# Identity products and split stores in the opening, attention-times-v in runs of two head pairs, and the first w3 columns converted during the attention

## The chip, the cores and the metric

The kernel runs on 1 core of a Trainium2 chip. The time is the device time of one execution in microseconds; the kernel before took 1345.91 us as the median of three runs.

## The reference

Inputs: q, k, v of 4 batches x 12 heads x 448 positions x 64, two 12 x 12 matrices that mix heads, and the weights of two layers.

```python
scores = scale * (q @ k.T)                      # per batch and head
scores = einsum('bhij,hg->bgij', scores, w_pre) # mix heads before the softmax
attn = softmax(scores, axis=-1)
attn = einsum('bhij,hg->bgij', attn, w_post)    # mix heads after it
x = (attn @ v) as [1792, 768]
h = ((x @ w1) * (x @ w2)) @ w3 @ w_out          # 768 -> 1024 -> 1024 -> 768
y = leaky(h @ w_in2) @ w_out2                   # 768 -> 2048 -> 768, slope 0.01
```

The weights come as 64-bit floats, read as pairs of 32-bit words and turned into 32-bit floats on the chip.

## The kernel before, in words

**Attention** (`attention`). 448 query positions of a batch are cut into chunks of 120, 120, 120 and 88 (`chunks`), 16 chunks in all (`order`). For a chunk, `qk` (line 199) makes the scores of six pairs of heads, three products a head from a high and a low part of q and k, and stores them to memory by four heads (`sdr`, lines 225 and 241). `relayout` (243) loads them back so that the partitions hold 5 positions x 12 heads: a group is two blocks of 10 positions, two loads. `premix` (253) mixes heads by a product with `kpre`; `softmax` (264) takes the maximum on VectorE and the exponential with its sum on ScalarE; `weigh` (275) scales the second mixing matrix by the reciprocal of the sum on GpSimd (`kr`); `postmix` (286) mixes and turns in one product, and its result is copied to `ap`. `av` (304) multiplies one pair of heads with v.

The loop `for k in range(NG + 1)` runs over 92 groups: 6 in a chunk of 120, 5 in a chunk of 88 (`t` counts them). Iteration k emits, in this order, the stores that are due, the softmax of group k, the post mix of group k - 1, the weighting of group k, the relayout of group k + 4 (`AHEAD`), the scores of a pair of heads two chunks ahead, products with v of the chunk that is complete (`todo`), and the pre mix of group k + 1. Behind them come the small works in `lows` (copies of y, low parts of q and k on VectorE), loads, and steps of `filler`. The order is written out by hand, and each engine, SP's queue of transfers among them, works through it in that order.

`todo` holds the six pairs of a complete chunk. Two are taken in its second iteration and, with 6 iterations, one in each further one. Three pairs share one PSUM bank ("px", one buffer), which a copy to `y` empties (line 324).

**Filler.** `conversions` (331) turns w_out into high and low 32-bit parts in memory (`wos`), in 16 units of 128 x 384: load, absolute value on ScalarE, four steps on VectorE, high part on ScalarE, low part on VectorE, store. From group 7 on each iteration takes one step, two at t = 2.

**Opening** (line 380 on). Loads of q and k, splits, the six `qk` of chunk 0 each with a `flush` of finished stores, four relayouts, the six `qk` of chunk 1, the first pre mix, then the loop.

**Expert layers** (`moe`, 469). `fold` multiplies w3 with w_out once (`w34`): 8 blocks of 128 columns of w3 (f), each 48 products, each block loaded as 64-bit words and converted (`next_w`, `ready_w`). Then two halves of the tokens go through w1, w2, w34, w_in2 and w_out2; TensorE is fed by the same loading and converting, two ahead. The tiles of this part lie in the memory of the attention's and wait for it to become free, tile by tile.

```python
left = nt - t if t else 1
for _ in range(-(-len(todo) // left)):
    av(*todo.pop(0))
```

Of the kernel before, what the change touches and what calls it, by code (L numbers as in the profile page):

```python
# [23 lines left out]
def attention_moe_kernel(ctx: ExitStack, tc, qt, kt, vt, w_pre, w_post, w1, w2, w3t, w_out, w_in2, w_out2, out):  # L24
# [38 lines left out]
    wos = dram.tile([DF, 2, DM], F32, name="wos")  # L63

# [25 lines left out]
    def convert_steps(pool, t, shape, bufs=2):  # L90

        c = pool.tile([P, *shape], U32, tag="wc", name="wc", bufs=bufs)
# [26 lines left out]
    def attention():  # L119
        with ExitStack() as es:  # L120
# [45 lines left out]
            kls, qls, stores = {}, {}, []  # L166
# [32 lines left out]
            def qk(b, c, p):  # L199
# [131 lines left out]
            def conversions():  # L331

                units = [(r, c0, DM // 2) for r in range(DF // P) for c0 in (0, DM // 2)]
                raws = []

                def load():
                    if units:
                        r, c0, n = units.pop(0)
                        words = w_out[r * P:(r + 1) * P, 2 * c0:2 * (c0 + n)].unsqueeze(1)
                        raws.append((load_raw(ws, words, (1, n), 3), wos[r * P:(r + 1) * P, :, c0:c0 + n], n))  # L340

                def begin():
                    t, dst, n = raws.pop(0)
                    return dst, *convert_steps(ws, t, (1, n), 3)
# [6 lines left out]
                while unit:  # L351
                    dst, cf, steps = unit
# [8 lines left out]
                    hl = ws.tile([P, 2, DM // 2], F32R, tag="hl", name="hl", bufs=1)  # L361
                    hi_act(hl[:, 0], cf[:, 0])
                    yield
                    lo_dve(hl[:, 1], cf[:, 0], hl[:, 0])
                    stores.append((dst, hl.bitcast(F32)))
# [35 lines left out]
            for k in range(AHEAD):  # L401
                relayout(k)
            for p in range(NPAIR):
                qk(0, 1, p)
                flush()
            q_split(0, 2)()
            premix(0)
            todo = []
            for k in range(NG + 1):
# [14 lines left out]
                if k < NG:  # L424
# [24 lines left out]
                if k < NG:  # L449
# [19 lines left out]
    def moe():  # L469
        with ExitStack() as es:  # L470
# [19 lines left out]
            def fold(unit):  # L490
# [47 lines left out]
            plan = [("w3t", f) for f in range(KF)]  # L538
# [15 lines left out]
            def next_w(ahead=2):  # L554
                while len(ready) < ahead and pos[1] < len(plan):
# [3 lines left out]
                    fill()  # L559
                return ready.pop(0)  # L560
# [140 lines left out]
```

## Time and profile before

| what | us |
|---|---|
| runs | 1346.77, 1345.91, 1343.42 (median 1345.91) |
| the profiled execution | 1345.55 |
| its span, first to last instruction | 1343.8 |
| TensorE products busy | 1312.6 (98%) |
| VectorE busy | 880.7 (66%) |
| ScalarE busy | 601.0 (45%) |
| GpSimd busy | 166.0 (12%) |

All times in rows are counted from the span's start. A row of a timeline gives start, duration, engine, line, operation, what is written from what, and a count where neighbours are merged; behind it stands the idle time before it and what ended it. PE is TensorE's products, PEld its weight loads, DVE VectorE, ACT ScalarE, POOL GpSimd, SPq the queue that issues transfers. A busy TensorE is not one at its peak, since its products overlap and their ends are modelled.

### The profile page before, as it was taken

What the parts mean: (1) busy time and instruction counts of PE and PEld (TensorE: products, weight loads), DVE (VectorE), ACT (ScalarE), POOL (GpSimd) and SP (SyncE); (2) the same over time, 40 slices, a digit from 0 to 9 for tenths busy, and PEclk for the clock granted to TensorE, in tenths of its full rate; (3) what the DMA queues carried; (4) which work ended last, traced back from release to release, by engine and by line L of the source; (5) the groups of instructions that cost most, each with busy time, mean ns of one, the idle gap of its engine ahead of it and who ended that gap; (6) DMA issues with size and microseconds to landing.
All of it is one profiled execution on the core that took longest, in us unless ns stands there. A gap on an engine that the chain in (4) does not pass through costs nothing.

```text
span 1343.8 us, 22895 instructions
## 1 busy us (share of the span) xinstructions
PE 1312.6 (98%) x8880; PEld 1124.0 (84%) x8880; DVE 880.7 (66%) x1519; ACT 601.0 (45%) x1163; POOL 166.0 (12%) x371
## 2 busy tenths in 40 slices
PE   6999999999999799999999999999999999999998
PEld 4676767666666799898989999999889899999998
DVE  5576676666666775763449587696674359596762
ACT  4665666666653443332226434252432235443240
POOL 1343444343334000000000000000000000000000
PEclk8999999999999899999999999999999999999999
DMA  7998988997888874331324342346331233342402
GB/s 231 307 281 254 277 275 258 286 299 216 271 278 265 271 232 158 99 106 48 102 94 146 104 150 72 117 125 228 94 101 57 84 113 118 118 137 81 136 1 82
DMA packets 138880, 224.19 MB, mean 167 GB/s; under 512 B 20052, under 2 KB 120404, under 8 KB 138324
## 3 DMA queue, kind: packets, MB, share of 16 engines
q1 hardware_dynamic: 138772, 222.73, 52.9%
q8 instruction: 70, 1.15, 0.4%
q14 instruction: 38, 0.31, 0.1%
HBM read 163.72 MB, written 58.98 MB: 166 GB/s over the span
## 4 chain that ended last, share of the span: by engine, by line
PE 87%; DMA 6%; DVE 2%; POOL 2%; ACT 1%; issue 1%; SPq 0%; POOLq 0%; ACTq 0%; DVEq 0%
PE pm L567 43%; PE po L636 17%; PE po L295 9%; PE px L315 5%; PE pw L505 5%; PE pm L260 4%; PE pq L215 4%; DMA sr<-sdr 1%; POOL kr L281 1%; DMA sdr<-s 1%; DMA ql<-in_q_dram 1%; DMA xm<-scr 1%; DMA wr<-in_moe_w_dram 1%; ACT e L270 1%; DVE mx L267 0%
## 5 line engine op out<-in xcount | busy, mean ns | idle before, releaser
L567 PE MATMUL pm<-x,ws 128*128 128x512 f32 (+1 forms) x2304 | 467.0, 364 | 0.3 <-ACT x L76 0.3
L567 PEld LDWEIGHTS pm<-x,ws 128*128 128x128 f32 x2304 | 417.6, 188 | 48.3 <-ACT x L76 0.7
L636 PE MATMUL po<-ws,g 128*128 128x384 f32 x1344 | 234.2, 334 | 0.0
L636 PEld LDWEIGHTS po<-ws,g 128*128 128x128 f32 x1344 | 233.1, 188 | 0.0
L295 PEld LDWEIGHTS po<-kr,e 128*112 128x112 f32 x1440 | 156.1, 178 | 71.3 <-POOL kr L281 33.1
L295 PE MATMUL po<-kr,e 128*112 128x120 f32 (+1 forms) x1440 | 175.7, 274 | 3.6 <-POOL kr L281 2.9
L270 ACT ACTIVATE e<-pm,mx 128x448 f32<-128x448 f32 x180 | 112.9, 632 | 145.1 <-DVE mx L267 145.1
L79 DVE TENSOR_TENSOR ws<-wc,ws 128x768 fp32r<-128x768 f32 (+1 forms) x104 | 101.5, 978 | 80.5 <-ACT ws L76 80.1
L95 ACT ACTIVATE wc<-wr 128x768 f32<-128x768 f32 (+2 forms) x120 | 104.5, 874 | 80.7 <-DVE ws L79 59.9
L76 ACT ACTIVATE ws<-wc 128x768 fp32r<-128x768 f32 (+1 forms) x104 | 89.3, 861 | 110.1 <-PE po L636 74.0
L267 DVE TENSOR_REDUCE mx<-pm 128x1 f32<-128x448 f32 x180 | 104.2, 619 | 43.2 <-PE pm L260 39.8
L281 POOL TENSOR_SCALAR kr<-kpost,rc 128x120 f32<-128x120 f32 x180 | 122.9, 683 | 66.9 <-DVE rc L279 62.2
L567 PE MATMUL pm<-h,ws 128*128 128x512 f32 (+1 forms) x576 | 116.3, 363 | 0.0
L567 PEld LDWEIGHTS pm<-h,ws 128*128 128x128 f32 x576 | 104.3, 188 | 11.7
L106 DVE SCALAR_TENSOR_TENSOR wc<-wr,wc 128x768 uint32<-128x768 uint32 (+2 forms) x120 | 110.2, 919 | 1.3
L103 DVE SCALAR_TENSOR_TENSOR wc<-wr,wc 128x768 uint32<-128x768 uint32 (+2 forms) x120 | 110.1, 919 | 1.2
L215 PE MATMUL pq<-ks,qs 64*120 64x448 f32 (+1 forms) x576 | 90.1, 419 | 10.1 <-ACT ks L76 5.6
L223 ACT ACTIVATE s<-pq 120x448 f32<-120x448 f32 (+1 forms) x180 | 88.5, 543 | 21.9 <-PE pq L215 20.8
L97 DVE TENSOR_SCALAR wc<-wc 128x768 f32<-128x768 f32 (+2 forms) x120 | 64.9, 541 | 50.1 <-ACT wc L95 49.9
L260 PE MATMUL pm<-sr,kpre 60*64 60x448 f32 x720 | 94.3, 571 | 3.3 <-DMA sr<-sdr 3.3
L315 PEld LDWEIGHTS px<-ap,vs 112*64 112x64 f32 x1536 | 73.9, 136 | 25.7 <-issue 17.3
L315 PE MATMUL px<-ap,vs 112*64 112x120 f32 (+1 forms) x1536 | 90.4, 264 | 3.6 <-DVE y L324 2.9
(51 smaller groups left out, 971.2 us busy)
## 6 DMA issues: line engine op xcount, KB each, us to landing
sr<-sdr SPq DMA_DIRECT2D x176, 210.0 KB
sdr<-s SPq DMA_DIRECT2D x36, 840.0 KB
wr<-in_moe_w_dram SPq DMA_DIRECT2D x32, 768.0 KB
wr<-in_moe_w_in_dram SPq DMA_DIRECT2D x32, 768.0 KB
wr<-in_moe_w_out_dram SPq DMA_DIRECT2D x32, 768.0 KB
wr<-in_moe_w_dram SPq DMA_DIRECT2D x8, 1024.0 KB
sdr<-s SPq DMA_DIRECT2D x12, 616.0 KB
wr<-in_moe_w_out_dram SPq DMA_DIRECT2D x16, 384.0 KB
```

What stands on the lines that cost most here:

```text
L95: nc.scalar.activation(out=cf, in_=hi.bitcast(F32), func=ACTF.Abs)
L103: lambda: nc.vector.scalar_tensor_tensor(out=c, in0=hi, scalar=0xC0000000, in1=c, op0=ALU.bitwise_and, op1=ALU.bitwise_or),
L106: lambda: nc.vector.scalar_tensor_tensor(out=c, in0=lo, scalar=29, in1=c, op0=ALU.logical_shift_right, op1=ALU.bitwise_or),
L215: nc.tensor.matmul(pq[e][:m], qst[b, c][rows, p, x, :m], kst[b, p][rows, y, :], start=(j == 0), stop=(j == 2))
L260: nc.tensor.matmul(pms[n][g * Q:(g + 1) * Q], kpre[rows], sr[rows, g, :], start=True, stop=True)
L267: nc.vector.tensor_reduce(out=mx, in_=pm, axis=AX.X, op=ALU.max, negate=True)
L270: ends["act"] = nc.scalar.activation(out=e, in_=pm, func=ACTF.Exp, bias=mx, scale=1.0, accum_out=sm)
L281: ends["pool"] = nc.gpsimd.tensor_scalar(out=kr, in0=kpost, scalar1=rc, scalar2=None, op0=ALU.mult)
L295: nc.tensor.matmul(po[:, jc].rearrange("p h (g i) -> p h g i", g=2), e[:, jc * JP:(jc + 1) * JP], kr, start=True, stop=True,)
L315: nc.tensor.matmul(px[e * D:(e + 1) * D, r, :ni], vst[b][:, jc, 2 * p + e, :], ap[:, jc, 2 * p + e, :ni], start=(jc == 0), stop=(jc == NJ ...
L567: nc.tensor.matmul(dst, wt[:, a, kk, :], x[:, kk, c, c0:c0 + w], start=(kk == 0 and j == 0), stop=(kk == kn - 1 and j == 2),)
L636: nc.tensor.matmul(po, g[:, m, a, t * P:(t + 1) * P], wts[m][:, c, 0, cs], start=(m == 0 and j == 0), stop=(m == FQ - 1 and j == 2),)
```

## The change

It makes the following changes. (1) `turn` issues products of the identity matrix with itself into the bank "px": 8 before the first scores, 3 behind each pair of heads of chunk 0, 2 behind each pair of chunk 1 and 6 at the end. (2) The three stores of chunk 0 are split in rows 0 to 59 and rows 60 to 119; the second halves are issued after three relayouts. (3) Two pairs of heads share the bank for the product with v, and both are taken in one iteration, at t = 1, 3 and 5 (1, 3 and 4 in a short chunk). (4) The filler gets three more units, the first 128 columns of w3 (3, 3 and 2 blocks of 128 rows), takes two steps at t = 4 too, and `fold` loads these columns ready-made from `w3s`; only one block is prepared ahead before the first one's products.

```diff
+    w3s = dram.tile([P, 2, DF // P, P], F32, name="w3s")
...
                     if r == HP - 1:
-                        stores.append((sdr[b, c][:, 2 * g * HP:2 * (g + 1) * HP, :], t[:m]))
+                        heads = slice(2 * g * HP, 2 * (g + 1) * HP)
+                        for i, r0 in enumerate((0, CH // 2) if first else (0,)):
+                            r1 = r0 + CH // 2 if first else m
+                            (behind if i else stores).append((sdr[b, c][r0:r1, heads, :], t[r0:r1]))
...
+            def turn(n):
+
+                t = bank("px", [P, P], "turn")
+                for _ in range(n):
+                    nc.tensor.matmul(t, ident, ident, start=True, stop=True)
...
-                g, r = divmod(p, 3)
+                g, r = divmod(p, 2)
...
-                    pxs[0] = bank("qa" if g and (b, c) == order[-1] else "px", [P, 3, CH], "px")
+                    pxs[0] = bank("qa" if g and (b, c) == order[-1] else "px", [P, 2, CH], "px")
...
-                if r == 2:
+                if r == 1:
                     copy = nc.scalar.copy if (b, c) == order[-1] else nc.vector.tensor_copy
-                    lows.append(lambda: copy(y[:, 3 * g:3 * g + 3, :ni], px[:, :, :ni]))
+                    lows.append(lambda: copy(y[:, 2 * g:2 * g + 2, :ni], px[:, :, :ni]))
...
-                units = [(r, c0, DM // 2) for r in range(DF // P) for c0 in (0, DM // 2)]
+                n = DM // 2
+                KW = n // P
+                units = [("out", r, c0) for r in range(DF // P) for c0 in (0, n)]
+                units += [("w3", min(KW, DF // P - k0), k0) for k0 in range(0, DF // P, KW)]
...
+            turn(8)
             for p in range(NPAIR):
                 qk(0, 0, p)
+                turn(3)
                 flush()
...
             for k in range(AHEAD):
+                if k == CH // (4 * IB):
+                    stores += behind
+                    flush()
                 relayout(k)
             for p in range(NPAIR):
                 qk(0, 1, p)
+                turn(2)
                 flush()
+            turn(6)
...
-                    left = nt - t if t else 1
-                    for _ in range(-(-len(todo) // left)):
-                        av(*todo.pop(0))
+                    if todo and (t % 2 or t == nt - 1):
+                        for _ in range(2):
+                            av(*todo.pop(0))
...
-                        for _ in range(2 if k >= START and t == 2 else 1):
+                        for _ in range(2 if k >= START and t in (2, 4) else 1):
                             next(filler, None)
...
-                        wt = next_w()
+                        if f:
+                            wt = next_w()
+                        else:
+                            wt = sp.tile([P, 2, KF, P], F32R, tag="ws", name="ws")
+                            nc.sync.dma_start(out=wt.bitcast(F32), in_=w3s)
+                            prepare(1)
...
-            plan = [("w3t", f) for f in range(KF)]
+            plan = [("w3t", f) for f in range(1, KF)]
```

`prepare(ahead)` is the loop of `next_w` without its last line.

## Rows read from the trace of the kernel before

**Rows 1.** The profile's page, part 4: chain that ended last, by line.

```profile
PE pm L567 43%; PE po L636 17%; PE po L295 9%; PE px L315 5%; PE pw L505 5%; PE pm L260 4%; PE pq L215 4%; DMA sr<-sdr 1%; POOL kr L281 1%; DMA sdr<-s 1%; DMA ql<-in_q_dram 1%; DMA xm<-scr 1%; DMA wr<-in_moe_w_dram 1%; ACT e L270 1%; DVE mx L267 0%
```

**Rows 2.** Stretches: length, busy of PE, PEld, DVE, ACT, POOL; clock; DMA share; GB/s.

```profile
19.00:20.00 1.00, 1.00 (x8) 1.00 (x7) 0.48 (x1) 0.43 (x2) 0.00 (x0) 1.00 0.96 401
...
22.00:23.00 1.00, 0.85 (x9) 0.46 (x5) 0.73 (x2) 0.82 (x2) 0.00 (x0) 1.00 0.00 0
...
27.00:28.00 1.00, 1.00 (x6) 0.00 (x0) 0.48 (x1) 0.00 (x0) 0.00 (x0) 0.50 1.06 224
```

**Rows 3.** Line 215, weight loads, 0 to 8 and 38 to 39.5 us; ns minimum/median/maximum.

```profile
L215 PEld LDWEIGHTS pq<-ks,qs x12: 271/313/322, 5.6 to 7.5; 64*120 64x120 f32 x12
...
L215 PEld LDWEIGHTS pq<-ks,qs x6: 176/178/179, 38.3 to 38.7; 64*120 64x120 f32 x6
```

**Rows 4.** Timeline of PE, 0 to 60 us.

```profile
25.73 5.10 PE L260 MATMUL pm<-sr,kpre 60*64 60x448 f32 x16 [2.88 <-DMA sr<-sdr]
30.76 3.54 PE L295 MATMUL po<-kr,e 128*112 128x120 f32 x16
```

**Rows 5.** Chain of waits, 0 to 60 us: start, us, what.

```profile
15.75 6.70 DMA sdr<-s
...
43.10 12.74 DMA sr<-sdr
```

**Rows 6.** Chain of waits over the span, the longest pieces.

```profile
60.13 1.79 PE px L315 x32
...
65.43 0.97 PE px L315 x16
```

**Rows 7.** Timeline of PE, pre mixes from 107 to 123 us.

```profile
107.55 0.98 PE L260 MATMUL pm<-sr,kpre 60*64 60x448 f32 x8
...
111.08 0.98 PE L260 MATMUL pm<-sr,kpre 60*64 60x448 f32 x8
...
116.42 0.98 PE L260 MATMUL pm<-sr,kpre 60*64 60x448 f32 x8
...
122.60 0.98 PE L260 MATMUL pm<-sr,kpre 60*64 60x448 f32 x8
```

**Rows 8.** Timeline, 83 to 90 us.

```profile
83.38 0.98 PE L260 MATMUL pm<-sr,kpre 60*64 60x448 f32 x8
...
84.31 1.22 POOL L281 TENSOR_SCALAR kr<-kpost,rc 128x120 f32<-128x120 f32 x1 [0.36 <-DVE rc L279]
...
89.18 0.98 PE L260 MATMUL pm<-sr,kpre 60*64 60x448 f32 x8
```

**Rows 9.** VectorE's groups by shape, 0 to 450 us: busy us, mean ns, idle before.

```profile
L324 DVE COPY y<-px 128x360 f32<-128x360 f32 x24 | 12.8, 532 | 15.3 <-PE px L315 15.3
L79 DVE TENSOR_TENSOR qs<-ql,qs 128x720 fp32r<-128x720 f32 x12 | 10.9, 908 | 5.6 <-ACT qs L76 5.4
...
L103 DVE SCALAR_TENSOR_TENSOR wc<-wr,wc 128x384 uint32<-128x384 uint32 x16 | 8.9, 553 | 0.1
```

**Rows 10.** Chain of waits, 415 to 470 us.

```profile
434.73 3.66 DMA wos<-hl
```

**Rows 11.** Timeline, 443 to 462 us.

```profile
443.32 2.79 SPq L241 DMA_DIRECT2D scr<-y  x1
...
444.46 3.86 PE L315 MATMUL px<-ap,vs 112*64 112x88 f32 x96 [0.65 <-DVE ap L302]
446.01 1.17 ACT L95 ACTIVATE wc<-wr 128x1024 f32<-128x1024 f32 x1 [4.54 <-DMA wr<-in_moe_w_dram]
...
453.17 1.65 PE L505 MATMUL pw<-wo,ws 128*128 128x384 f32 x4 [4.84 <-ACT ws L76]
...
456.34 6.07 PE L505 MATMUL pw<-wo,ws 128*128 128x384 f32 x18 [1.53 <-ACT ws L76]
```

**Rows 12.** Stretches in the fold, columns as in rows 2.

```profile
457.00:462.00 5.00, 5.00 (x18) 5.00 (x17) 4.49 (x7) 2.70 (x4) 0.00 (x0) 0.50 1.06 341
466.00:470.00 4.00, 4.00 (x25) 4.00 (x24) 3.42 (x4) 2.96 (x5) 0.00 (x0) 1.00 0.90 289
```

More of the change, by code (lines that the diff above doesn't have):

```diff
@@ L88, in load_raw, with convert_steps @@
         return t.rearrange("p k (m two) -> p k m two", two=2)
-    def convert_steps(pool, t, shape, bufs=2):
-        c = pool.tile([P, *shape], U32, tag="wc", name="wc", bufs=bufs)
+    def convert_steps(pool, t, shape, bufs=2, room=None):
+        c = pool.tile([P, *(room or shape)], U32, tag="wc", name="wc", bufs=bufs)
+        if room:
+            c = c[:, 0, :shape[0] * shape[1]].rearrange("p (k m) -> p k m", k=shape[0])
         hi, lo = t[:, :, :, 1], t[:, :, :, 0]
@@ L164, in constants @@
                 )
-            kls, qls, stores = {}, {}, []
+            kls, qls, stores, behind = {}, {}, [], []
             kst, vst, qst, st = {}, {}, {}, {}
@@ L331, in conversions @@
             def conversions():
-                units = [(r, c0, DM // 2) for r in range(DF // P) for c0 in (0, DM // 2)]
+                n = DM // 2
+                KW = n // P
+                units = [("out", r, c0) for r in range(DF // P) for c0 in (0, n)]
+                units += [("w3", min(KW, DF // P - k0), k0) for k0 in range(0, DF // P, KW)]
                 raws = []
                 def load():
[L337 to L340, printed above, removed]
+                    if not units:
+                        return
+                    kind, r, c0 = units.pop(0)
+                    t = ws.tile([P, 2 * n], U32, tag="wr", name="wr", bufs=3)
+                    if kind == "out":
+                        nc.sync.dma_start(out=t, in_=w_out[r * P:(r + 1) * P, 2 * c0:2 * (c0 + n)])
+                        shape = (1, n)
+                    else:
+                        t = t[:, :2 * r * P]
+                        words = w3t[c0 * P:(c0 + r) * P, :2 * P].rearrange("(k p) m -> p k m", p=P)
+                        nc.sync.dma_start(out=t.rearrange("p (k m) -> p k m", k=r), in_=words)
+                        shape = (r, P)
+                    raws.append((kind, r, c0, shape, t.rearrange("p (k m two) -> p k m two", k=shape[0], two=2)))
                 def begin():
-                    t, dst, n = raws.pop(0)
-                    return dst, *convert_steps(ws, t, (1, n), 3)
+                    kind, r, c0, shape, t = raws.pop(0)
+                    return (kind, r, c0), *convert_steps(ws, t, shape, 3, (1, n))
                 for _ in range(2):
@@ L351, in conversions @@
                 while unit:
-                    dst, cf, steps = unit
+                    (kind, r, c0), cf, steps = unit
                     unit = None
@@ L360, in conversions @@
                         yield
-                    hl = ws.tile([P, 2, DM // 2], F32R, tag="hl", name="hl", bufs=1)
-                    hi_act(hl[:, 0], cf[:, 0])
+                    hl = ws.tile([P, 2, n], F32R, tag="hl", name="hl", bufs=1)
+                    w = cf.shape[1] * cf.shape[2]
+                    cf = cf.rearrange("p k m -> p (k m)")
+                    hi_act(hl[:, 0, :w], cf)
                     yield
-                    lo_dve(hl[:, 1], cf[:, 0], hl[:, 0])
-                    stores.append((dst, hl.bitcast(F32)))
+                    lo_dve(hl[:, 1, :w], cf, hl[:, 0, :w])
+                    if kind == "out":
+                        dst = wos[r * P:(r + 1) * P, :, c0:c0 + n]
+                    else:
+                        dst = w3s[:, :, c0:c0 + r, :].rearrange("p x k m -> p x (k m)")
+                    stores.append((dst, hl[:, :, :w].bitcast(F32)))
                     yield
@@ L498, in fold @@
                             behind.enter_context(tc.issue_after(e.ins))
-                        wt = next_w()
+                        if f:
+                            wt = next_w()
+                        else:
+                            wt = sp.tile([P, 2, KF, P], F32R, tag="ws", name="ws")
+                            nc.sync.dma_start(out=wt.bitcast(F32), in_=w3s)
+                            prepare(1)
                     for hf in range(2):
@@ L552, in fill, with prepare @@
                     pos[0] += 1
-            def next_w(ahead=2):
+            def prepare(ahead):
                 while len(ready) < ahead and pos[1] < len(plan):
@@ L559, in next_w @@
                     fill()
+            def next_w(ahead=2):
+                prepare(ahead)
                 return ready.pop(0)
```

## The prediction

> **What bounds the kernel now.** I read the chain of work that ended last first. By line it is TensorE nearly everywhere: the products of the expert layers (lines 567, 636, 505) hold 65% of the span and the attention's products (295, 315, 260, 215) 22% [rows 1]. The change does not touch the expert layers behind the fold, so what it can win or lose lies in three places: the opening (0 to 56 us), the attention's loop (56 to 443 us) and the handing over to the fold (443 to 466 us).
>
> *Opening.* By the microsecond [rows 2] the DMA engines move 401 GB/s while the first chunk's scores go out, move nothing at 22 to 23 us, and work fully again at 27 us, where the granted clock is 0.50, the lower level of 1.2 GHz. The weight loads of the first scores last 313 ns, against 178 ns at 38 us [rows 3]: TensorE was at the lower level from its first product, though the clock column shows 1.00 there. It then sat idle 2.88 us for the first relayout [rows 4]. The chain runs through transfers: the last store of the first chunk (15.75 us) takes 6.70 us to land, and a relayout issued at 43.10 us takes 12.74 us, up to 55.84 us [rows 5]. A 215 KB load with so long a way lies behind others in the queue: up to 56 us the queue sets the pace, whatever TensorE does.
>
> *Loop.* An iteration without a product with v takes 111.08 - 107.55 = 3.53 us, one with two pairs 116.42 - 111.08 = 5.34 us [rows 7]; one pair alone adds 0.97 us, two in a run 1.79 us [rows 6]. So TensorE sets the pace, unless the chain maximum, exp, sum, reciprocal, weighting is late.
>
> *Fold.* TensorE starts its last products with v at 444.46 us and is done 3.86 us later; the converted w3 columns let it go on at 456.34 us [rows 11]. It works at half clock then: 18 products in 5 us (278 ns each), against 25 in 4 us (160 ns) at the full 2.4 GHz [rows 12].
>
> The profiled execution took 1345.55 us (span 1343.8 us and 1.75 us around it); the median of the three runs, 1345.91 us, is 0.36 us above it. The sum is made on 1345.55 us. About 0.3%, 4 us, is what a measurement of this kernel can tell from no change.
>
> **The opening, step by step.** Each first store is 120 rows x 4 heads x 448 x 4 bytes, 0.86 MB; three of them precede the first relayout, and half of that, 1.29 MB, now goes behind the third relayout. At 401 GB/s [rows 2] this is 3.2 us, so the first relayout may start at about 22.45 - 3.2 = 19.2 us. The row of a 0.39 MB store gives the same: it lands 3.66 us after its issue [rows 10], and the last half is issued near 15.5 us. But the 3.2 us are moved, not saved: they now lie between relayouts 2 and 3. Relayout 3 reads rows 60 to 79, which belong to the later half, so SP waits there until those stores have landed, and behind it in SP's order stand relayout 3, the stores of the second chunk, every further relayout, and the loads of v and w_out. The queue runs dry a second time, as it does at 22 to 23 us: one slice of 1 us is empty [rows 2], and with the tail before it and the start behind it (pre mix 3.3 us after the landing at 22.45 us [rows 4, 5]) I take 2 us, between 1 and 3.3 us. At the relayout that ended at 55.84 us: -3.2 + 3.2 + 2.0 = **+2.0 us**.
>
> Identity products: 8 + 6x3 + 6x2 + 6 = 44, each an fp32 product of 128 columns. No row shows one; the nearest is the post mix, 16 instructions for 8 products in 3.54 us at half clock, 0.44 us each [rows 4], and by the weight loads' ratio 178/313 about 0.25 us at full clock. The first 8 (3.5 us) run while TensorE waits for the first keys (5.6 us, [rows 3]). The scores of both chunks took at most 25.73 - 2.88 - 5.6 = 17.25 us; at full clock about 9.8 us, and 36 identity products add 9.0 us: the first pre mix could start near 24.4 us instead of 25.73 us. This cover is the queue's: since the transfers set the time at 56 us, I put the earlier start and the better clock at nothing. The gain would be real if the queue were not the limit; the full end for it is below, in the first rival.
>
> **The loop.** Per chunk the runs were one of two and four of one, 1.79 + 4x0.97 = 5.67 us; three runs of two are 5.37 us: -0.30 us for 11 of the chunks. In three of the short chunks (5 iterations) two single pairs met in one iteration, the second waiting for the copy out of the only bank: 122.60 - 116.42 = 6.18 us [rows 7]. Pairing by twos avoids that: I put 1.0 us on each. The last chunk wins about 0.7 us. Together -7.0 us.
>
> Against it stands VectorE's order. The copy of y waits for the run's last product, and what is queued behind it waits too: the low part of q (0.91 us) and a conversion step (0.55 us) [rows 9], then the maxima of the next iteration. That one has now no product with v to hide behind. The nearest row is an iteration where a key split fell into VectorE's late stretch: one weighting on GpSimd took 1.22 us, and the iteration 89.18 - 83.38 = 5.80 us instead of 5.34 us, 0.46 us lost [rows 8]. I charge about 0.5 us once for the seven chunks whose q split falls on such a place (3.4 us), half of it twice for the three chunks with key splits there (1.4 us), 1.6 us for the chunk that has no scores to compute any more, whose two added light iterations end before their own chain does, and 1.0 us for the third conversion of w3, now in iterations 2 and 4. Extra copies of y (three of 240 columns for two of 360, at 0.53 us each for 360) are within these. Sum +7.4 us, net **+0.4 us**. Bounds: -7.0 us if nothing is late, +9.5 us if every place costs.
>
> **The fold.** By the count of calls (116 are needed, 116 come) the last w3 step falls on the end of the last full iteration, where y is copied and its store issued at 443.32 us [rows 11]. The last store of w3s then goes out near 444 us and lands 3.3 us later (a somewhat larger one takes 3.66 us [rows 10]); the load of all columns, 1.05 MB, needs 3.1 us at 341 GB/s [rows 12] and about 2 us for issue and landing: TensorE starts near 452.5 us instead of 456.34 us. It had 4 products done before; with 278 ns until 462 us and 160 ns after, the first columns ended at 465.8 us before (20 at half clock, 24 at full) and end at 464.3 us after (34 and 14). The second columns' raw words cannot come earlier, since their buffer lies where the conversion's was: landing near 455.5 us, and the conversion of the first took 456.34 - 446.01 = 10.3 us beside the second's [rows 11], so at worst 465.8 us. I take 464.3: **-1.5 us**; bounds -5 us (the clock stays up and no wait) and +5 us (three raw loads of 3.1 us each ahead of w3s, less what the ready second columns give back).
>
> **Sum:** 1345.55 + 2.0 + 0.4 - 1.5 = 1346.45, rounded 1346.5 us: no change that a measurement can tell. With partial misses in the three terms this case reaches from 1342 to 1349.5 us.
>
> **Rivals.**
> 1. *TensorE, not the queue, sets the opening* (27%). For it: the idle 2.88 us and ten us at the lower clock. Against it: 12.74 us for a small load. Then 2.9 us of idle time and some 2.6 us of the half-clock stretch are won, -5.5 us in place of +2.0 us; with most of the loop's waits not coming, 1338 us.
> 2. *VectorE's queue decides the loop* (15%, slower). Place: the copy of y at iterations 1, 3 and 5, ahead of everything else. Price 0.5 us [rows 8] at three places in 11 chunks, 16.5 us, less 7.0 us: +9.5 us, so 1355.5 us. It decides once VectorE reaches the next maxima over 0.3 us later than TensorE's pre mix.
> 3. *Half the partitions, half the rate* (12%). The relayouts, each to 60 partitions, move 224 GB/s at 27 us, the stores from 120 partitions 401 GB/s [rows 2]. If partitions, not piece size, make that difference, the 1.29 MB behind takes 5.8 us, 2.6 us more: 1349.1 us, half of it on the slower side. The Trainium skill (SBUF — State Buffer, Door 1: The DMA port swizzle) says that the rate follows how many ports the partitions reach, and that partitions 0 to 63 reach half of them. By that rule the split would cost these 2.6 us; the two rows agree with it but differ in piece size as well.
> 4. *The identity products do not hold the clock* (8%): TensorE waits for relayouts 3 and 4 and falls back. By the queue's argument the time stays, 1346.5 us.
>
> The forecast itself has 38%. Faster: rival 1, 0.27. Same: 0.38 + 0.08 + 0.06 = 0.52. Slower: 0.15 + 0.06 = 0.21. The range 1337 to 1352.5 us holds all but rival 2 and the outer part of rival 1.
>
> **What would show it.** Right: weight loads of the first scores near 178 ns; the first relayout issued near 19.2 us; a second dry slice of the DMA near 30 us; the eighth pre mix not before 57 us; light iterations of 3.5 us and pairs of 5.3 us, with waits on the weighting after some; the fold's first product near 452.5 us. Wrong: a pre mix of 51 us there (rival 1), iterations of 4 us and more without a product with v (rival 2), or a fold that waits for its second columns.

## The result, and the profile of the changed kernel

The changed kernel takes 1358.58 us (median of 5 runs, 1357.7 to 1360.38) against 1344.47 us for the kernel before in the same comparison: ratio 1.0101, 95% interval 1.0085 to 1.0116. It is slower by 1%; the forecast was no change, and the time lies above its range. The profiled execution took 1357.95 us (span 1356.1 us, 12.3 us more than before).

Where the 12.3 us arose is read from the starts of the pre mixes in both timelines (below, "pre mix 7" is the eighth, that of iteration 7; "the loop" runs from it to the last pre mix).

| stretch | before | changed | difference | forecast |
|---|---|---|---|---|
| opening: pre mix 7 starts at | 55.88 | 62.27 | +6.4 | +2.0 |
| loop | 383.06 | 386.19 | +3.1 | +0.4 |
| last pre mix to the end | 904.86 | 907.64 | +2.8 | -1.5 |

**TensorE's groups** over the span, the changed kernel (busy us, mean ns, idle time before them and what ended it), products first, then the weight loads of 5 to 17 us:

```profile
L307 PE MATMUL po<-kr,e 128*112 128x120 f32 (+1 forms) x1440 | 179.1, 275 | 11.1 <-POOL kr L293 9.9
L547 PE MATMUL pw<-wo,ws 128*128 128x384 f32 x384 | 68.8, 340 | 10.6 <-ACT ws L77 10.0 <-DVE ws L80 0.6
L253 PE MATMUL turn<-ident 128*128 128x128 f32 x88 | 15.3, 318 | 1.5 <-POOL ident masks.py:199 1.5
...
L218 PEld LDWEIGHTS pq<-ks,qs 64*120 64x120 f32 x40 | 3.1, 178 | 2.4 <-ACT qs L77 0.6 <-ACT ks L77 0.6 <-DVE ks L182 0.5
```

The weight loads of the first scores last 178 ns: the identity products do hold the upper clock there, against 313 ns in [rows 3]. They cost 15.3 us of TensorE for 44 products: 3.8 us for the eight ahead of the scores and 0.32 us for each of the other 36. The post mix waits 9.9 us for the weighting on GpSimd, and the fold 10 us for its columns.

**The opening** by stretches (length, clock, DMA share, GB/s): first the kernel before, then the changed one.

```profile
12.00:33.00 21.00, 0.82 0.81 239
13.00:18.00 5.00, 1.00 0.92 271
19.00:21.00 2.00, 1.00 0.83 348
```

```profile
12.00:33.00 21.00, 1.00 0.69 187
13.00:18.00 5.00, 1.00 0.87 204
19.00:21.00 2.00, 1.00 0.03 11
27.00:31.00 4.00, 1.00 0.87 328
31.00:33.00 2.00, 1.00 0.13 28
```

From 12 to 33 us the changed kernel moves 21 x (239 - 187) = 1.09 MB less, which at the 321 GB/s of its next nine microseconds is 3.4 us of queue. The queue is dry at 19 to 21 us and again at 31 to 33 us, and the first halves move at 204 GB/s although the DMA engines are busy. SP's own queue shows the two waits (issue, time to the last issue of the group), and below it the end of the attention:

```profile
11.85 4.44 SPq L247 DMA_DIRECT2D sdr<-s  x3
20.51 2.64 SPq L261 DMA_DIRECT2D sr<-sdr  x6
23.20 2.57 SPq L247 DMA_DIRECT2D sdr<-s  x3
31.82 0.79 SPq L261 DMA_DIRECT2D sr<-sdr  x2
32.73 2.19 SPq L247 DMA_DIRECT2D sdr<-s  x3
...
437.02 17.35 SPq L247 DMA_DIRECT2D w3s<-hl  x2
454.42 0.61 SPq L247 DMA_DIRECT2D scr<-y  x1
456.42 2.58 SPq L88 DMA_DIRECT2D wr<-in_moe_w_dram  x3
459.05 4.23 SPq L540 DMA_DIRECT2D ws<-w3s  x1
```

SP stands from 25.8 to 31.8 us at relayout 3; the second chunk's stores, issued at 26.27 us before, go out at 32.73 us. At the end the last store of the converted w3 columns keeps SP until 454.4 us, and three raw loads precede the load of those columns, although in the kernel's text that load stands ahead of `prepare(1)`, which issues them.

**TensorE's timeline** of the changed kernel at the places that answer to [rows 4, 7, 11] (start, duration, idle time before it):

```profile
27.42 1.72 PE L272 MATMUL pm<-sr,kpre 60*64 60x448 f32 x12
...
45.36 2.91 PE L272 MATMUL pm<-sr,kpre 60*64 60x448 f32 x8 [4.16 <-DMA sr<-sdr]
48.20 3.54 PE L307 MATMUL po<-kr,e 128*112 128x120 f32 x16
...
71.70 0.98 PE L272 MATMUL pm<-sr,kpre 60*64 60x448 f32 x8
...
77.00 0.98 PE L272 MATMUL pm<-sr,kpre 60*64 60x448 f32 x8
...
80.51 0.98 PE L272 MATMUL pm<-sr,kpre 60*64 60x448 f32 x8
...
83.36 1.07 PE L307 MATMUL po<-kr,e 128*112 128x120 f32 x8 [0.81 <-POOL kr L293]
...
454.65 3.86 PE L327 MATMUL px<-ap,vs 112*64 112x88 f32 x96 [0.65 <-DVE ap L314]
468.48 1.01 PE L547 MATMUL pw<-wo,ws 128*128 128x384 f32 x2 [9.97 <-ACT ws L77]
470.12 6.11 PE L547 MATMUL pw<-wo,ws 128*128 128x384 f32 x26 [0.64 <-DVE ws L80]
```

TensorE waits 4.16 us for relayout 4, and the post mix behind it takes 3.54 us, as long as at half clock in [rows 4]; the granted clock reads 0.50, the level of 1.2 GHz, at 44 to 45 us, when TensorE is idle, and still at 48 to 49 us. Pairs take 77.00 - 71.70 = 5.30 us and light iterations 3.51 us, as forecast. The fold starts at 468.48 us, with products of its second columns.

**VectorE**, then GpSimd, at 77 to 83 us:

```profile
77.12 0.41 DVE L336 COPY y<-px 128x240 f32<-128x240 f32 x1 [0.78 <-PE px L327]
77.44 0.90 DVE L80 TENSOR_TENSOR qs<-ql,qs 128x720 fp32r<-128x720 f32 x1
78.26 0.55 DVE L106 SCALAR_TENSOR_TENSOR wc<-wr,wc 128x384 uint32<-128x384 uint32 x1
78.72 1.15 DVE L279 TENSOR_REDUCE mx<-pm 128x1 f32<-128x448 f32 x2
...
81.84 0.62 DVE L182 TENSOR_TENSOR ks<-kl,ks 128x448 fp32r<-128x448 f32 x1
82.38 0.55 DVE L109 SCALAR_TENSOR_TENSOR wc<-wr,wc 128x384 uint32<-128x384 uint32 x1
```

```profile
82.09 1.22 POOL L293 TENSOR_SCALAR kr<-kpost,rc 128x120 f32<-128x120 f32 x1 [0.36 <-DVE rc L291]
```

VectorE stands 0.78 us for the last product with v, and only then does the low part of q and the filler's step; the maxima start 1.72 us behind their pre mix (77.00 us). A weighting beside two-input work of VectorE then takes 1.22 us instead of 0.59 us.

### The profile page after: what moved, and what is told of

It is laid out like the page before. It is cut to its first block, busy times and chain, and to the rows that moved or that the text cites. A ratio compares the mean times of both kernels' runs of the same rounds, so it can differ in the third digit from the quotient of the medians.

```text
span 1356.1 us, 23088 instructions
## 1 busy us (share of the span) xinstructions
PE 1319.4 (97%) x8968; PEld 1130.4 (83%) x8968; DVE 883.3 (65%) x1544; ACT 599.6 (44%) x1168; POOL 161.6 (12%) x371
## 4 chain that ended last, share of the span: by engine, by line
PE 86%; DMA 4%; POOL 3%; DVE 2%; ACT 2%; issue 1%; SPq 0%; POOLq 0%; ACTq 0%; DVEq 0%
PE pm L612 43%; PE po L681 17%; PE po L307 7%; PE pw L547 5%; PE px L327 5%; PE pq L218 4%; PE pm L272 4%; POOL kr L293 2%; DMA sr<-sdr 2%; ACT e L282 1%; DMA sdr<-s 1%; DVE mx L279 1%; PE turn L253 1%; DMA wr<-in_moe_w_dram 1%; POOL sm L289 1%
## 5 line engine op out<-in xcount | busy, mean ns | idle before, releaser
L307 PE MATMUL po<-kr,e 128*112 128x120 f32 (+1 forms) x1440 | 179.1, 275 | 11.1 <-POOL kr L293 9.9
L98 ACT ACTIVATE wc<-wr 128x768 f32<-128x768 f32 (+3 forms) x122 | 104.9, 862 | 84.7 <-DVE ws L80 63.2
L293 POOL TENSOR_SCALAR kr<-kpost,rc 128x120 f32<-128x120 f32 x180 | 118.4, 658 | 67.8 <-DVE rc L291 61.3
L109 DVE SCALAR_TENSOR_TENSOR wc<-wr,wc 128x768 uint32<-128x768 uint32 (+3 forms) x122 | 110.6, 907 | 1.4
L106 DVE SCALAR_TENSOR_TENSOR wc<-wr,wc 128x768 uint32<-128x768 uint32 (+3 forms) x122 | 110.6, 908 | 1.4
L100 DVE TENSOR_SCALAR wc<-wc 128x768 f32<-128x768 f32 (+3 forms) x122 | 65.2, 534 | 56.7 <-ACT wc L98 56.5
L218 PE MATMUL pq<-ks,qs 64*120 64x448 f32 (+1 forms) x576 | 86.4, 397 | 3.8 <-ACT s L226 2.5
L314 DVE COPY ap<-po 112x480 f32<-112x480 f32 (+1 forms) x136 | 87.4, 643 | 2.9 <-PE po L307 2.9
```

The lines of the kernel that those rows point to most:

```text
L98: nc.scalar.activation(out=cf, in_=hi.bitcast(F32), func=ACTF.Abs)
L106: lambda: nc.vector.scalar_tensor_tensor(out=c, in0=hi, scalar=0xC0000000, in1=c, op0=ALU.bitwise_and, op1=ALU.bitwise_or),
L109: lambda: nc.vector.scalar_tensor_tensor(out=c, in0=lo, scalar=29, in1=c, op0=ALU.logical_shift_right, op1=ALU.bitwise_or),
L218: nc.tensor.matmul(pq[e][:m], qst[b, c][rows, p, x, :m], kst[b, p][rows, y, :], start=(j == 0), stop=(j == 2))
L293: ends["pool"] = nc.gpsimd.tensor_scalar(out=kr, in0=kpost, scalar1=rc, scalar2=None, op0=ALU.mult)
L307: nc.tensor.matmul(po[:, jc].rearrange("p h (g i) -> p h g i", g=2), e[:, jc * JP:(jc + 1) * JP], kr, start=True, stop=True,)
```

## Experiments

Times are medians, with the ratio to the kernel before in the same comparison; its own median lay between 1343.87 and 1345.56 us.

The diffs show the main lines of each edit, shortened.

**One part undone each.** Stores whole again; no identity products; runs of three pairs again; no w3 part:

```diff
e1: -(behind if i else stores).append(...)      +stores.append((sdr[b, c][:, ...], t[:m]))
e2: -turn(8)  -turn(3)  -turn(2)  -turn(6)
e3: -g, r = divmod(p, 2)                        +g, r = divmod(p, 3)
e4: -units += [("w3", ...)]  -t in (2, 4)       +t == 2
```

> The changed kernel with whole first stores again (all 120 rows in one store, ahead of every relayout); identity products kept. Theory A (the wait of SP for the later half of the stores opens a second gap in the transfers, and TensorE idles and loses its clock behind it): no second dry stretch, relayout 4 lands some 10 us earlier, no half clock after 43 us, the pre mix of iteration 7 starts at 55 to 56 us instead of 62.3, and the time is about 1358.6 - 6.4 = 1352 us. Theory B (the identity products themselves delay the first iterations): pre mix of iteration 7 stays near 62 us, time 1358 to 1359 us. If TensorE and not the queue set the opening before, it starts at 50 to 53 us and the time is 1347 to 1349 us.

> The changed kernel without the 44 identity products; split stores kept. Theory A (the split's wait): the gap stays, pre mix of iteration 7 at 61 to 64 us, time 1357 to 1361 us, and the weight loads of the first scores last 313 ns again. Theory B (the identity products delay the first iterations): pre mix of iteration 7 near 56 us, time about 1352 us.

> The changed kernel with the product with v dealt as before (banks of three pairs, one pair in most iterations), the filler's second step in iterations 2 and 4 kept. Theory A (the light iterations, in which VectorE is late with q's and k's low parts, cost more than runs of two save): the loop from pre mix 7 to 87 is 2 to 3 us shorter, time about 1356 us; idle time of the post mix for the weighting on GpSimd falls from 9.9 us to 3 to 5 us. Theory B (the filler's second step in iteration 4 alone makes the loop longer): no difference, 1358 to 1359 us, idle time for the weighting stays at 8 to 10 us.

> The changed kernel with the w3 part undone: the fold's first columns are converted after the attention again, the filler has 16 units and a second step in iteration 2 only. Theory A (the filler that lasts to the end holds the buffers back, so that the raw w3 loads go late and ahead of the ready columns): the raw loads are issued before the last products with v, the fold's first product starts about 12 us after those products as before, and the handing over is 2.8 us shorter; with about 1 us of the loop for the steps that are gone, 1354.5 to 1356 us. Theory B (the ready columns are worth something, and the loss lies elsewhere): 1358 us or more.

| run | time us | ratio (interval) | pre mix 7 | loop |
|---|---|---|---|---|
| e1 no split | 1354.29 | 1.0071 (1.0056 to 1.0086) | 57.74 | 387.96 |
| e2 no identity products | 1359.73 | 1.0108 (1.0093 to 1.0123) | 60.08 | 386.12 |
| e3 runs of three | 1357.86 | 1.0102 (1.0085 to 1.0120) | 62.81 | 384.92 |
| e4 no w3 part | 1350.10 | 1.0042 (1.0027 to 1.0057) | 62.52 | 382.50 |

At pre mix 7 the split costs 62.27 - 57.74 = 4.5 us (60.08 - 55.88 = 4.2 us without identity products), the identity products 57.74 - 55.88 = 1.9 us. In e1 the clock is up, but relayout 0 is issued at 23.47 us instead of 22.59 us, and TensorE waits 2.21 us for the relayout of iteration 7, then works at half clock; TensorE in e1, and SP's queue in e2:

```profile
57.74 1.64 PE L269 MATMUL pm<-sr,kpre 60*64 60x448 f32 x8 [2.21 <-DMA sr<-sdr]
59.30 3.54 PE L304 MATMUL po<-kr,e 128*112 128x120 f32 x16
```

```profile
19.16 2.64 SPq L261 DMA_DIRECT2D sr<-sdr  x6
31.65 1.25 SPq L247 DMA_DIRECT2D sdr<-s  x3
```

So the better clock is given back in iteration 7, and the division depends on where it is read. One pre mix later (61.85 us before, 68.19 changed, 65.34 in e1, 65.81 in e2) the sum is the same 6.3 us, but the split has 2.9 us of it (4.0 us without identity products) and the identity products 3.5 us. In the whole time e1 is 4.3 us below the changed kernel and e2 not below it: that taking out the identity products shortens the changed kernel is not shown. In the loop the runs of two alone gain 0.6 us (e4), the w3 steps alone cost 1.9 us (e3), both together 3.1 us. In e3 the post mix waits 3.6 us for the weighting, and up to iteration 87 the loop is 3.0 us shorter, as theory A had it; but the last chunk, where runs of two win, gives 1.8 us back, and the time hardly moves. The w3 part costs 8.5 us in all, 3.7 us of it in the loop, so e4's expectation was too small; e1's time lies between its two theories, and e2 has the time of its theory A, with pre mix 7 a little earlier (60.08 us, 61 to 64 expected).

**Second step of the filler moved; old opening; copies last.** e5 moves the second step to the iterations with a product with v; e6 is e5 without split and identity products; e8 is e6 with VectorE's copy of y issued behind the low parts and the filler's steps:

```diff
e5: -for _ in range(2 if k >= START and t in (2, 4) else 1):
    +for _ in range(2 if k >= START and t % 2 else 1):
e8: -lows.append(lambda: copy(y[...], px[...]))
    +copies.append(lambda: copy(y[...], px[...]))
     next(filler, None)
    +while copies:
    +    copies.pop(0)()
```

> The changed kernel with one thing moved: the filler's second step in the iterations with a product with v (1, 3, 5) instead of 2 and 4. The filler then needs 116 calls of about 126 and ends some seven iterations before the attention does. Theory A (loop: the second step in the light iterations 2 and 4 stretches the weighting; fold: a filler that lasts to the very end frees its buffers late and so puts three raw loads ahead of the ready columns): the loop from pre mix 7 to the last one takes 382 to 383 us instead of 386.2, the raw loads and the load of the ready columns are issued before the last products with v, the fold's first product comes within 2 us behind them, and the time is 1342 to 1349 us. Theory B (the load order at the fold is the scheduler's own and the end of the filler has no part in it): the fold's gap of 10 us stays, and only the loop gains: 1354 to 1356 us. Theory C (more steps beside products with v delay the copy of y or the scores): no gain in the loop, 1357 us or more.

> The same with the opening of the kernel before (whole first stores, no identity products). If opening, loop and fold add up: 6.4 us less than the run with the second step at 1, 3 and 5, so 1336 to 1343 us, below the kernel before. If the loop takes up what the opening gives (a wait that is hidden otherwise): 1344 us or more.

> The version with the second step at 1, 3 and 5 and the old opening, and with the copy of y issued on VectorE behind the low parts of q and k and the filler's steps instead of ahead of them. Theory A (VectorE stands at the copy, and what is queued behind it is late): the idle time of the post mix for the weighting falls below 4 us, and the time is 2 to 4 us less than that of the version with the copy ahead, 1333 to 1340 us. Theory B (VectorE's work in those iterations is too much in any order): within 1 us of that version.

e5: 1362.34 us, 1.0124 (1.0109 to 1.0139). e6: 1355.15 us, 1.0067 (1.0044 to 1.0091). e8: 1338.32 us, 0.9951 (0.9933 to 0.9969). TensorE's post mix in e6, in e8, and VectorE in e8:

```profile
L304 PE MATMUL po<-kr,e 128*112 128x120 f32 (+1 forms) x1440 | 180.4, 275 | 14.2 <-POOL kr L290 12.9
```

```profile
L304 PE MATMUL po<-kr,e 128*112 128x120 f32 (+1 forms) x1440 | 178.7, 276 | 4.3 <-POOL kr L290 3.0
```

```profile
71.07 0.91 DVE L80 TENSOR_TENSOR qs<-ql,qs 128x720 fp32r<-128x720 f32 x1
...
72.48 0.56 DVE L109 SCALAR_TENSOR_TENSOR wc<-wr,wc 128x384 uint32<-128x384 uint32 x1
72.95 0.40 DVE L333 COPY y<-px 128x240 f32<-128x240 f32 x1
73.27 1.15 DVE L276 TENSOR_REDUCE mx<-pm 128x1 f32<-128x448 f32 x2
```

Theory C of e5 held: more steps behind a copy that waits lengthen the loop to 391.92 us; theory A, 1342 to 1349 us, fell. The same steps ahead of the copy run while TensorE still works on the product with v (70.31 to 72.17 us); the copy then waits for nothing, and the maxima start 1.17 us behind their pre mix (72.10 us) although one step more stands there. Order alone is worth 391.65 - 378.64 = 13.0 us of loop between e6 and e8, and 16.8 us of the whole time: theory A of e8 held, with a far larger gain than its 2 to 4 us. e6 is 7.2 us below e5, about what the opening had cost. At the fold e5 has its gap nearly closed (1.36 and 0.34 us idle, 2.0 us later on), but the time went elsewhere: the conversions, now early, stand on VectorE ahead of the last copy of the post mix's result, and TensorE waits for that copy:

```profile
464.66 5.30 PE L327 MATMUL px<-ap,vs 112*64 112x88 f32 x96 [3.44 <-DVE ap L314]
471.33 0.61 PE L547 MATMUL pw<-wo,ws 128*128 128x384 f32 x2 [1.36 <-ACT ws L77]
```

**The copy's place by itself, and w3 in the mended order.** e9 is the changed kernel, e10 the kernel before, each with copies last only; e11 is e8 without the w3 part; e12 is e8 with one line to keep the conversions behind that last copy:

```diff
e12: -copy(ap[:, :, :, o:o + nb], po)
     +done = copy(ap[:, :, :, o:o + nb], po)
     +if copy is nc.vector.tensor_copy:
     +    ends["dve"] = done
```

> The changed kernel as it is (identity products, split stores, second step in iterations 2 and 4), with the copy of y issued on VectorE behind the low parts and the filler's steps of its iteration. Theory A (the place of the copy on VectorE is what costs the loop time): idle time of the post mix for the weighting falls from 9.9 to below 4 us, the loop from pre mix 7 to the last one takes 379 to 381 us instead of 386.2, opening and fold stay as they are, and the time is 1352 to 1354 us. Theory B (the place of the copy matters only where the second step stands in the same iteration, as in the version measured; in the changed kernel the light iterations themselves are too full): 1357 us or more, idle for the weighting above 7 us.

> The kernel before, with only the copy of y issued behind the low parts and the filler's step. Theory A (before, an iteration with one pair hides the wait for the copy, so its place is worth little; the gain needs the runs of two): 1343 to 1346.5 us, no difference that can be told. Theory B (the place of the copy alone makes the gain, whatever the runs): 1338 to 1341 us.

> The version with the copies last, the second step at 1, 3 and 5 and the old opening, without the w3 part (fold's first columns converted after the attention, second step in iteration 2 only). Theory A (with VectorE's order mended the w3 steps cost the loop nothing and the ready columns save the gap at the fold, 1.4 us instead of 8 us, and its half clock): 1343 to 1346 us, 5 to 8 us above the same with the w3 part. Theory B (the steps cost in the loop what the fold gives): within 1.5 us of 1338.3 us or below it.

> The version with the copies last, the second step at 1, 3 and 5 and the old opening, and the fold's first conversions on VectorE kept behind the last copy of the post mix's result, where they stand ahead of it (the last products with v wait 2.8 us for that copy, and last 5.5 us instead of 3.9). Theory A (that wait is on the path): idle time before the last products with v falls to about 0.7 us, the attention ends 2 to 4 us earlier, 1334.5 to 1336.5 us. Theory B (the conversions of the second columns are then as much later, and the fold waits for them): within 1 us of 1338.3 us.

e9: 1353.50 us, 1.0058 (1.0043 to 1.0072), loop 380.00 us, wait for the weighting 5.2 us instead of 9.9 us (I expected under 4). e10: 1342.09 us, 0.9982 (0.9971 to 0.9993), loop 383.27 us, unchanged: the wait for the weighting fell from 2.9 to 1.7 us, that for the copy of y rose from 2.9 to 5.1 us; what it gained, between its two theories, lies behind the loop. e11: 1340.31 us, 0.9959 (0.9945 to 0.9973), loop 379.67 us. So with copies last the runs of two do save 383.27 - 379.67 = 3.6 us of the loop in these two traces (5.2 us from pre mix 8 on, since e11's iteration 7, behind a wait of 1.01 us for its relayout, falls to half clock); the whole times are 1.8 us apart. Without the w3 part e11 is 2.0 us above e8, between the two theories, but the intervals overlap: what the w3 part is worth there is not told apart from nothing. e12: 1337.28 us, 0.9940 (0.9927 to 0.9954); the line did not move the conversions (TensorE still waits 2.37 us there), so it tells nothing of that wait and serves as a second run of e8.

**The opening once more.** e7 is the kernel before with eight identity products ahead of the first scores and none between; e13 the changed kernel with relayout 3 behind the second chunk's stores on SP, e14 the same order in e8, with split stores and no identity products. e17 and e18 are the kernel before with each first store cut in two, by heads (120 partitions) or by rows (60 partitions), both sent at once:

```diff
e13: -for k in range(AHEAD): relayout(k)
     +for k in range(AHEAD - 1): relayout(k)
     +stores += behind; flush()
      for p in range(NPAIR): qk(0, 1, p); turn(2); flush()
     +relayout(AHEAD - 1)
e17: +for h0, h1 in ((0, 2), (2, 4)):
     +    stores.append((sdr[b, c][:, 4 * g + h0:4 * g + h1, :], t[:m, h0:h1]))
e18: +for r0, r1 in ((0, 60), (60, 120)):
     +    stores.append((sdr[b, c][r0:r1, heads, :], t[r0:r1]))
```

> The kernel before with eight identity products ahead of the first scores, and none between them. Theory A (the queue sets the opening, and TensorE's work between the scores only delays the first stores): the weight loads of the first scores fall from 313 to about 178 ns, the third store is issued at 12.5 to 14 us instead of 16, the first relayout at 19 to 21 us instead of 22.6, and the pre mix of iteration 7 at 53 to 55 us: 1342 to 1344 us. Theory B (without work between the scores the clock falls again while they wait for keys and evictions): weight loads again above 250 ns in part, and the time is that of the kernel before within 1 us, 1344 to 1346 us.

> The changed kernel with the relayout that has to wait for the later halves issued behind the second chunk's stores on SP instead of ahead of them. Theory A (the split costs through what is queued behind SP's wait): no dry stretch at 31 us, iterations 3 and 4 take 3.5 to 5 us each instead of 7.8 and 7.7, pre mix of iteration 7 at 57 to 59 us instead of 62.3, time 1353.5 to 1356 us. Theory B (the moved bytes themselves, half the partitions at half the rate): pre mix of iteration 7 stays at 61 us or later, 1357 us or more.

> The version with the copies last and the second step at 1, 3 and 5, with the split stores in that mended order on SP and no identity products. Theory A (the first relayouts come 2 to 3 us earlier, but up to the pre mix of iteration 7 the queue sets the time): first pre mix at 22 to 23 us, pre mix of iteration 7 at 55 to 58 us, time within 2 us of 1338.3 us. Theory B (with the wait gone the earlier start is a gain): pre mix of iteration 7 at 51 to 54 us, 1334 to 1336 us.

> The kernel before with each of the first chunk's three stores cut in two by heads: 120 partitions, 0.43 MB each, sent as soon as the heads are ready, no other change. Theory A (the number of partitions that a store comes from sets its rate): the stores move at 300 to 400 GB/s once several are under way, first relayout issued at 22 to 23.5 us, time that of the kernel before within 2 us. Theory B (stores of half the size are slower whatever partitions they reach): 200 to 240 GB/s, first relayout at 25 us or later, 1347 us or more.

> The kernel before with each of the first chunk's three stores cut in two by rows, 60 partitions each, both halves sent one right after the other, in the order of before; no identity products. Theory A (60 partitions have half the rate, store by store): 200 to 240 GB/s from 12 us on, the last half landed some 4 to 6 us later, first relayout at 26 to 29 us, time 1347 to 1350 us. Theory B (the rate follows the partitions of all stores in flight; with both halves under way together it is that of whole stores): 300 to 400 GB/s, first relayout at 22 to 24 us, time of the kernel before within 2 us.

| run | time us | ratio (interval) | pre mix 7 |
|---|---|---|---|
| e7 eight identity products | 1343.88 | 0.9994 (0.9981 to 1.0006) | 55.92 |
| e13 relayout 3 later | 1358.87 | 1.0110 (1.0094 to 1.0127) | 61.48 |
| e14 e8 with split | 1342.81 | 0.9986 (0.9977 to 0.9995) | 62.26 |
| e17 cut by heads | 1343.17 | 0.9991 (0.9981 to 1.0001) | 54.71 |
| e18 cut by rows | 1343.74 | 0.9987 (0.9975 to 0.9999) | 54.98 |

e7: the eight alone don't hold the clock (weight loads of 278 ns mean at 5 to 25 us, the products back at half speed). e13 by stretches and on TensorE:

```profile
12.00:33.00 21.00, 1.00 0.80 219
31.00:33.00 2.00, 1.00 0.87 294
```

```profile
42.18 2.73 PE L272 MATMUL pm<-sr,kpre 60*64 60x448 f32 x8 [4.43 <-DMA sr<-sdr]
```

The dry stretch at 31 us is gone, three fifths of the missing bytes are back (219 against 187 and 239 GB/s), and the time is the same. Theory A fell: relayout 3 now lands behind the second chunk's stores, and TensorE waits 4.43 us for it instead of 4.16 us for relayout 4. Whichever goes first, one is late; before, relayouts 0 to 3 all stood ahead of those stores. e14 shows the same in the mended kernel: 4.5 us dearer than e8, with a wait of 7.27 us, and both its theories fell. e13's numbers are those of theory B, but that theory took 60 partitions to have half the rate. The stretches of e17, then of e18:

```profile
13.00:18.00 5.00, 1.00 0.88 289
```

```profile
13.00:18.00 5.00, 1.00 0.90 285
```

Cut either way, stores sent together move as fast as whole ones (271 GB/s before), if a little under the 300 GB/s expected, and the time is that of the kernel before. Number and size of the stores, and 60 partitions in each, are therefore not the cost; having the halves apart is. The gap is wider behind the first two microseconds: at 15 to 18 us whole stores move 330 GB/s, e18's 344 GB/s, the changed kernel's 209 GB/s.

**Ready columns ahead of the raw loads**, in the changed kernel (e15) and in e8 (e16):

```diff
-nc.sync.dma_start(out=wt.bitcast(F32), in_=w3s)
-prepare(1)
+first = nc.sync.dma_start(out=wt.bitcast(F32), in_=w3s)
+with tc.issue_after(first.ins):
+    prepare(1)
```

> The changed kernel with the load of the ready columns issued ahead of the three raw loads of w3. Theory A (the order of the loads makes the gap): the ready columns land 2 to 8 us earlier, the fold starts with 48 products of the first columns at 461 to 465 us instead of 468.5, waits then for the second ones, and the time is 1355 to 1358 us. Theory B (the late buffers make it: the second columns come as late or later, and TensorE waits for them instead): 1358 us or more.

> The version with the copies last, the second step at 1, 3 and 5 and the old opening, with the load of the ready columns ahead of the raw loads. Theory A (the ready columns wait for nothing but their place in the order): the waits for them at the fold, 1.4 to 2.5 us, go, 1335.5 to 1338 us. Theory B (their buffer comes free only with the end of the attention, and the raw loads, moved behind them, are then late): TensorE waits for the second columns by 5 us or more, 1341 us or more.

e15: 1354.14 us, 1.0068 (1.0054 to 1.0082). e16: 1336.90 us, 0.9944 (0.9932 to 0.9957). TensorE in e15, then in e16:

```profile
460.86 10.19 PE L548 MATMUL pw<-wo,ws 128*128 128x384 f32 x48 [3.22 <-DMA ws<-w3s]
472.78 0.96 PE L548 MATMUL pw<-wo,ws 128*128 128x384 f32 x4 [1.73 <-ACT ws L77]
```

```profile
444.73 8.60 PE L540 MATMUL pw<-wo,ws 128*128 128x384 f32 x48 [1.05 <-DMA ws<-w3s]
456.93 0.96 PE L540 MATMUL pw<-wo,ws 128*128 128x384 f32 x4 [3.60 <-ACT ws L77]
```

One issue moved is worth 1358.58 - 1354.14 = 4.4 us in the changed kernel: the gap of 9.97 us becomes 3.22 us and 1.73 us. Theory A of e15 held, with a time 0.9 us below its range. In e16 the raw loads are late (issued at 444.62 us) and TensorE waits 3.60 us for the second columns, so both halves of e16's theories came true in part; against e8 the 1.4 us are not told apart. e16 is 0.6% below the kernel before: runs of two, copies last, filler's second step beside products with v, ready columns first, the old opening. e8, e11 and e12 are below both kernels too, by 0.4 to 0.6%, and the four are not told apart.

## Why the prediction was wrong

1. *Opening, +2.0 forecast, +6.4 measured.* Two steps failed. The identity products, put "at nothing" as covered by the queue, took 0.32 us each behind the scores instead of 0.25 us, so that the first pre mix came at 27.42 us and not near 24.4 us; with them and whole stores relayout 0 was issued 0.9 us later, and pre mix 7 started 1.9 us and pre mix 8 3.5 us later (e1). And "I take 2 us" for the second dry stretch was too little: the split by itself costs 4.2 us at pre mix 7 and 4.0 us at pre mix 8 (e2), with the second chunk's stores issued at 31.65 us instead of 26.27 us and TensorE waiting 4.64 us for relayout 4. The start worked out for the first relayout, 19.2 us, came true in e2 (19.16 us), in part by luck: 401 GB/s was the best single microsecond, while whole stores moved 271 GB/s at 13 to 18 us and the first halves by themselves 204 GB/s (205 GB/s in e2). In the changed kernel it was 20.51 us, with the identity products. The step "moved, not saved" was right (e14). Rival 3 gave the split 4.6 us in all, and 4.2 to 4.5 us came at pre mix 7, but not by its mechanism as stated: the later halves, alone at 27 to 31 us, moved at 328 GB/s. By the port rule of the Trainium skill that it named (SBUF — State Buffer, Door 1: The DMA port swizzle) both halves would be slow; the trace agrees for the first and not for the second. How the split's microseconds divide between the two dry stretches, the slow first halves and the half clock is open.
2. *Rival 1* (TensorE sets the opening) fell as far as the kernel tests it: e1 has the upper clock and pre mix 7 is 1.9 us later. But the clock is held there by products that themselves fill TensorE up to the first pre mix.
3. *Rival 4* was right in "TensorE waits for relayouts 3 and 4 and falls back" and wrong in "by the queue's argument the time stays" as far as iterations go: those of 3 and 4 took 7.76 and 7.71 us instead of 3.5 us. By rows at either level the lower clock made up some 2.2 us of iteration 4: the post mix took 3.54 us instead of 1.90 us, the scores behind it 1.47 us instead of 0.88 us.
4. *Loop, +0.4 forecast, +3.1 measured*, inside its bounds. Without the w3 steps the working gives +0.4 - 1.0 = -0.6 us, and e4 measured -0.6 us; this checks the sum and not each of its terms. The mis-sized term is "1.0 us for the third conversion of w3": the w3 steps cost 3.7 us (changed kernel against e4). That iteration 4 is light and already holds low parts of q and k may be why, but e5, which moved the step out of it, was no shorter; with the copies last and the steps beside products with v they cost the loop nothing (378.64 us in e8, 379.67 us without them in e11).
5. *Rival 2* named the place rightly, the copy "ahead of everything else": moving it is worth 6.2 us of the changed kernel's loop (e9) and 13.0 us with the steps beside it (e6, e8). Its price, 16.5 us, was too high for the changed kernel. In the forecast the place stood as something given; it was one line to move, and most of the gain of the runs of two hung on it.
6. *Fold, -1.5 forecast, +2.8 measured* (0.7 us of it still ahead of the last products with v). The step that failed is "TensorE starts near 452.5 us", 4.2 us behind the end of those products: it was 9.97 us. The step took the store's landing for the only thing ahead of the load, and three raw loads stood between, as the upper bound had it. A filler that runs to the very end made those loads late, but did not put them first: in e5 and e8, where they go out before the attention ends, the load of the ready columns still goes out behind them (at 469.24 and 447.24 us). With that load first, 2.8 - 4.4 = -1.6 us, near the forecast; that the ready columns brought it is not shown, since in e4, without them, the last pre mix to the end takes 903.08 us, already 1.8 us less than before, and 902.51 us in e15.

## What to carry to other kernels

Work on an in-order engine that does not need the running product belongs ahead of the instruction that waits for it: here the place of one copy decided whether the same regrouping of products saved 0.6 us or 3.6 us of the loop. Cutting a transfer so that an early reader can start did not help here, where the queue was the bound; it only chose who was late (e13, e14). When work is made ready in advance, see that its last step, its buffers and its load don't end behind the loads that it was to replace.

## What the runs showed of the hardware that I had not expected

The first 60 rows of the score tile, stored alone, moved at 204 GB/s with the DMA engines 87% busy (205 GB/s in e2, 208 GB/s in e14); the other 60 rows, alone at 27 to 31 us, at 328 GB/s; both sent together at 285 GB/s, as whole stores do. Why the two halves differ is not shown. The Trainium skill (SBUF — State Buffer, "Can I just issue two DMAs to hit both halves?") says that transfers to the two halves of the partitions gain hardly anything by being under way together. Here 204 and 328 GB/s one behind the other would give 251 GB/s, so the 285 GB/s of e18 are 13% more, in one trace.

The upper clock came with the identity products between the scores and not with eight ahead of them: in e7 the weight loads of the scores that follow last 312 ns in the median at 6 to 22 us, though the granted clock in the profile's column reads 1.00 from 5 to 27 us. The durations tell the level there, the column does not.
